# The high words of the weights written to PSUM by VectorE, their low parts added there, and the second group's pieces dealt out anew

## The chip, the cores and the metric

The kernel runs on one core of a Trainium2 chip. The metric is device microseconds of one execution; the time before is 1161.85 us, the median of 3 runs (1161.53 to 1161.90). Engines are called TensorE (PE, its weight loads PEld), VectorE (DVE), ScalarE (ACT), GpSimd (POOL) and SyncE (SP).

## The reference

A dynamic convolution of 7 taps with softmax weights, and behind it a two-layer net with a squared relu. All inputs are float32; the weights of the net come as float64 words (the kernel reads them as pairs of 32-bit words).

```python
w = softmax(weight_gen, axis=-1)                 # (4, 4096, 8 heads, 7 taps)
x = sum over taps k of w[..., k] * x[s - 6 + k]  # per head of 24 of the 192 columns
h = x.reshape(16384, 192) @ w_in                 # (16384, 2048)
out = (s * relu(h) ** 2 + b) @ w_out             # (16384, 192)
```

## The kernel before

The 16384 rows are worked in 32 groups of 512. Float32 accuracy is had from fp32r products: each operand is split into a high part, rounded to fp32r, and a low part, and three products (high x high, high x low, low x high) are added in PSUM.

**The weights.** They lie in 8 chunks (`wc_0` to `wc_7`), each with 256 rows of the hidden layer: 768 columns of `w_in` and `w_out`, high and low part. `load_weights(i)` brings the raw 64-bit words to a tile `r` (4 buffers). `convert(i)` is a generator of four steps, each started by `ahead(i, 1)`:
1. ScalarE takes the absolute value of the high words (L220);
2. VectorE clamps it, shifts it and puts the float32 together in place, in the high words (L223, L227, L231); ScalarE copies that to the high part `hi` (L235);
3. VectorE reads the high words again for the exponent (L238) and makes `v`, what the 64-bit word has beyond the high word, from the low words (L242);
4. TensorE adds three products with identity matrices in the PSUM tile `h1`: the float32 as it is (L252, a float32 product, which takes two passes in the trace), minus `hi` (L253), plus `v` (L254); ScalarE copies the sum to the low part `lo` (L255).

**The first group.** Its convolution has pieces of its own (row layout, ahead of the rest). Its net is worked in eight half-steps i = 0 to 7 (the loop at L671), while the weights are still being converted. A half-step issues: `mm1_pair` of chunk i on TensorE (into the PSUM tile `h0`), `relu2` on ScalarE (L546 relu, L548 square, L552 the high part `gh`) with step 4 of conversion i + 1 between the square and `gh`, steps 2 and 3 of conversion i + 2, step 1 of conversion i + 3, `mm2_pair` of chunk i - 1 on TensorE (L586), some pieces of the second group's convolution on VectorE (the table `beside`), and `low_g` on VectorE (L558, the low part `gl`, which `mm2_pair` of the next half-step reads).

**The second group's pieces** (`conv_pieces(1)`): softmax (three pieces), four products of taps with weights (L403, two heads by taps 0 to 3 and 4 to 6), five additions (L414, the last L422) that sum the 7 taps, the transposes (L433, L438), the split into high part (L445) and low part (L451). `split_lo` also issues a transfer within SBUF (`xb`).

**The other groups.** From `mm1_quad(4)` on (L693 and below) four steps to a group: `mm1_quad` (L535), `relu2`, `mm2_quad` of the step before (L604), pieces of the group after next, `low_g`, and once a group `scale` (L616, L622), which empties the sums `po` to `y`.

Every engine's work is issued in the order in which it is written (`manual_schedule`); an engine's instructions run in that order, and the program sets semaphores where one waits for another. PSUM tiles `h0` and `h1` have one buffer each.

The lines that set the order of the stage:

```python
beside = ((0, 1), (1, 3), (3, 4), (4, 5), (5, 7), (7, 8), (8, 14), (14, 15))
for i in range(NC):
    mm1_pair(n, p, ...)
    relu2(n, [p], lambda: ahead(i + 1, 1))
    ahead(i + 2, 2)
    ahead(i + 3, 1)
    mm2_pair((i - 1) // 2, (i - 1) % 2)
    run_pieces(1, *beside[i])
    low_g(n, p)
```

Of the kernel before, what the change touches and what calls it, by code (L numbers as in the profile page):

```python
# [7 lines left out]
F32 = mybir.dt.float32  # L8
F32R = mybir.dt.float32r
U32 = mybir.dt.uint32  # L10
AF = mybir.ActivationFunctionType
ALU = mybir.AluOpType
# [8 lines left out]
def dynamic_conv_then_relu2_mlp(  # L21
# [24 lines left out]
    nc = tc.nc  # L46
# [3 lines left out]
    P = 128  # L50
# [6 lines left out]
    T = 512  # L57
# [153 lines left out]
    def convert(i):  # L211


        r = raw_t.pop(i)
        hi, lo = wc[i][:, 0], wc[i][:, 1]
        low_w, high_w = r[:, :, 0], r[:, :, 1]
        fv = high_w.bitcast(F32)
        t = (rows if i % 2 else raw).tile([P, CW], U32, tag="t", name="t", bufs=1)
        tv = t.bitcast(F32)
        nc.scalar.activation(out=tv, in_=fv, func=AF.Abs)  # L220
        yield

        nc.vector.tensor_scalar(  # L223
            out=tv, in0=tv, scalar1=LEAST, scalar2=MOST, op0=ALU.max, op1=ALU.min
        )

        nc.vector.tensor_scalar(  # L227
            out=t, in0=t, scalar1=3, scalar2=0x3FFFFFFF,
            op0=ALU.logical_shift_left, op1=ALU.bitwise_and,
        )  # L230
        nc.vector.scalar_tensor_tensor(  # L231
            out=high_w, in0=high_w, scalar=0xC0000000, in1=t,
            op0=ALU.bitwise_and, op1=ALU.bitwise_or,
        )
        nc.scalar.copy(out=hi, in_=fv)  # L235
        yield

        nc.vector.tensor_scalar(  # L238
            out=t, in0=high_w, scalar1=0xFF800000, scalar2=None, op0=ALU.bitwise_and
        )  # L240
        v = raw.tile([P, CW], F32R, tag="v", name="v", bufs=2)
        nc.vector.scalar_tensor_tensor(  # L242
            out=v, in0=low_w, scalar=2.0 ** -52, in1=tv, op0=ALU.mult, op1=ALU.mult
        )
        yield

        ps = ps_h.tile([P, 2, T], F32, tag="h1", name="ph")
        n = CW // 2
        for a in range(2):
            c = slice(a * n, (a + 1) * n)  # L250
            o = ps[:, a, 0:n]
            nc.tensor.matmul(out=o, lhsT=eye_f, rhs=fv[:, c], start=True, stop=False)  # L252
            nc.tensor.matmul(out=o, lhsT=neg_eye, rhs=hi[:, c], start=False, stop=False)  # L253
            nc.tensor.matmul(out=o, lhsT=eye, rhs=v[:, c], start=False, stop=True)  # L254
        nc.scalar.copy(out=lo.rearrange("p (a n) -> p a n", a=2), in_=ps[:, :, 0:n])  # L255
        yield

    def awake():
# [46 lines left out]
    def conv_pieces(g):  # L305
# [110 lines left out]
                )  # L416
            return f

        def last_add():
            pr = st["pr"]  # L420
            acc = small.tile([P, J, FQ], F32, tag="acc", name="acc", bufs=1)
            nc.vector.tensor_tensor(out=acc, in0=pr[:, 0], in1=pr[:, 2], op=ALU.add)  # L422
            st["acc"] = acc
            xt_t.pop(g)

# [37 lines left out]
        if g == 0:  # L463
            return [
                softmax_a, exp, softmax_b, row_tails(0), row_tails(1), row_tails(2), row_tails(3), row_hi(1),
                row_firsts(0, 2), row_firsts(2, 4), row_firsts(4, 6), row_firsts(6, 7), row_hi(0), row_lo,
            ]
        return [
            softmax_a, exp, softmax_b,
# [72 lines left out]
    def relu2(n, ps=(0, 1), between=None):  # L542
        r = {}
        for p in ps:
            r[p] = act.tile([P, 2, T], F32, tag="r", name="r")
            nc.scalar.activation(out=r[p], in_=h_t.pop((n, p)), func=AF.Relu)  # L546
        for p in ps:
            nc.scalar.activation(out=r[p], in_=r[p], func=AF.Square)  # L548
            if between:
                between()  # L550
            gh = gp.tile([P, 2, T], F32R, tag="gh", name="gh")
            nc.scalar.copy(out=gh, in_=r[p])  # L552
            g_t[n, p] = r[p], gh
# [89 lines left out]
    with tc.manual_schedule():  # L643
        constants()
        nc.scalar.activation(out=bias[:, 0:1], in_=ones_f[:, 0:1], func=AF.Exp)
        load_rows(0)
        for i in range(4):
            load_weights(i)
        load_gen(1)

        parts = [convert(i) for i in range(NC)]

        def ahead(i, n):
            for _ in range(n if i < NC else 0):
                next(parts[i])

        awake()
        run_pieces(0, 0, 8)
        ahead(0, 1)
        run_pieces(0, 8, 13)  # L660
        ahead(0, 2)
        load_weights(4)
        load_x(1)
        nc.sync.dma_start(out=s_sb, in_=s.partition_broadcast(P))
        nc.sync.dma_start(out=b_sb, in_=b.partition_broadcast(P))
        run_pieces(0, 13, 14)
        ahead(1, 1)
        ahead(0, 1)

        beside = ((0, 1), (1, 3), (3, 4), (4, 5), (5, 7), (7, 8), (8, 14), (14, 15))  # L670
        for i in range(NC):  # L671
            n, p = divmod(i, 2)
            mm1_pair(n, p, (0, 2, 1) if i < 2 else (0, 1, 2))
            if i == 0:
                ahead(2, 1)
                ahead(1, 2)
                load_weights(5)
            relu2(n, [p], lambda: ahead(i + 1, 1))
            ahead(i + 2, 2)
            if i + 6 < NC:  # L680
                load_weights(i + 6)
            ahead(i + 3, 1)
            if i == NC - 1:
                sums = column_sums()
            if i > 0:
                mm2_pair((i - 1) // 2, (i - 1) % 2)
            run_pieces(1, *beside[i])
            if i == NC - 1:
                set_bias(sums)
            low_g(n, p)  # L690
            if i == 4:
                load(2)
        run_pieces(2, 0, 3)  # L693
        last = NG * NQ - 1
        for n in range(NQ, last + 1):
            g, k = divmod(n, NQ)
            if k == 0 and g + 2 < NG:
                load(g + 2)
            if k == 3:
                zeros_before(g + 2)  # L700
            mm1_quad(n)
            relu2(n)
            mm2_quad(n - 1, (1,) if n == NQ else (0, 1))
            a = (3, 5), (5, 8), (9, 14), (0, 2)
            run_pieces(g + 1 + k // 3, *a[k])
            if n == NQ:
                scale(0, (0, 2))
            low_g(n, 0)
            if k == 0 and n > NQ:
                scale(g - 1, (0, 2))  # L710
            low_g(n, 1)
            if k == 0:
                scale(g - 1, (1, 3))
                store(g - 1, 0, NT)
            a = (5, 5), (8, 9), (14, 15), (2, 3)
            run_pieces(g + 1 + k // 3, *a[k])

        for t in range(NT):
            mm2_pair(last, 0, [t], t == NT - 1)
        for t in range(NT):  # L720
            mm2_pair(last, 1, [t], t == NT - 1)
            scale(NG - 1, [t])
            store(NG - 1, t, t + 1)
# [30 lines left out]
```

## Time and profile before

| | us |
|---|---|
| median of 3 runs | 1161.85 |
| the profiled execution | 1160.27 |
| its span, first to last instruction | 1158.6 |
| TensorE busy in the span | 1146.5 (99%) |
| VectorE | 931.2 (80%) |
| ScalarE | 828.2 (71%) |
| GpSimd | 38.8 (3%) |

The shares are means over the whole span, of which the first 85 us or so hold the start, the conversions and the first group; the rest is the repeated steps of the other groups. The chain that ended last lies on TensorE for 97% of the span, most of it in L604 (47%) and L535 (45%); L252 has 1.0%. The granted TensorE clock is 0.998 of full speed (2.4 GHz).

### The profile page before, as it was taken

The numbers are of one execution on the slowest core, as the hardware profiler recorded it, in microseconds if no ns is written. First come the engines' busy times: TensorE is split into PE (matmuls) and PEld (weight loads), VectorE is DVE, ScalarE is ACT, GpSimd is POOL, SyncE is SP. The second block draws the span as 40 slices with busy tenths as digits, with TensorE's granted clock in tenths as the row PEclk, the third lists the DMA queues.
The fourth block names the chain that finished last, engine by engine and source line by source line (L and its number), as shares of the span: only waits on it lengthen the run. The fifth ranks groups of instructions, "written<-read, shape, count | busy, mean of one in ns | idle before, by whom it ended". The sixth has DMA issues, their size and how long they took to land.

```text
span 1158.6 us, 30256 instructions
## 1 busy us (share of the span) xinstructions
PE 1146.5 (99%) x12752; PEld 1128.9 (97%) x12752; DVE 931.2 (80%) x1356; ACT 828.2 (71%) x894; POOL 38.8 (3%) x86
## 2 busy tenths in 40 slices
PE   8999999999999999999999999999999999999997
PEld 6789999999999999999999999999999999999997
DVE  8998888877888877889877889877889877889843
ACT  5867677677677677677677777677777677776674
POOL 8300000000000000000000000000000000000000
PEclk9999999999999999999999999999999999999999
DMA  8422212222212222212222212222212222211110
GB/s 205 98 45 35 45 26 37 47 46 35 47 25 37 48 47 33 47 25 37 47 47 34 47 25 37 47 48 34 46 26 37 47 47 33 47 27 36 24 25 14
DMA packets 171867, 50.38 MB, mean 43 GB/s; under 512 B 160788, under 2 KB 164500, under 8 KB 171732
## 3 DMA queue, kind: packets, MB, share of 16 engines
q1 hardware_dynamic: 169684, 47.40, 22.5%
q8 instruction: 100, 1.64, 0.6%
q0 software_dynamic: 2048, 1.05, 0.4%
q14 instruction: 35, 0.29, 0.1%
HBM read 27.70 MB, written 12.58 MB: 35 GB/s over the span
## 4 chain that ended last, share of the span: by engine, by line
PE 97%; DMA 1%; DVE 1%; ACT 0%; POOL 0%; issue 0%; POOLq 0%
PE po L604 47%; PE ph L535 45%; PE po L586 2%; PE ph L517 2%; PE ph L252 1%; DMA r<-in_moe_w_in_dram 1%; POOL r L195 0%; PE ph L254 0%; PE ph L286 0%; PE ph L253 0%; ACT gh L552 0%; DVE u L616 0%; DVE y L622 0%; ACT r L548 0%; DVE gl L558 0%
## 5 line engine op out<-in xcount | busy, mean ns | idle before, releaser
L604 PE MATMUL po<-wc,gh 64*128 64x384 f32 x3952 | 584.0, 354 | 0.3 <-DVE y L622 0.3
L604 PE MATMUL po<-wc,gl 64*128 64x192 f32 x3952 | 573.3, 247 | 0.0
L604 PEld LDWEIGHTS po<-wc,gh 64*128 64x128 f32 x3952 | 568.2, 184 | 0.7 <-PE po L604 0.5
L604 PEld LDWEIGHTS po<-wc,gl 64*128 64x128 f32 x3952 | 564.4, 187 | 0.1
L558 DVE TENSOR_TENSOR gl<-r,gh 128x1024 fp32r<-128x1024 f32 x256 | 313.0, 1223 | 202.8 <-ACT gh L552 197.3
L546 ACT ACTIVATE r<-ph 128x1024 f32<-128x1024 f32 x256 | 249.2, 1024 | 293.8 <-PE ph L535 259.4
L535 PE MATMUL ph<-xa,wc 64*128 64x512 f32 x2976 | 381.3, 391 | 0.0
L535 PEld LDWEIGHTS ph<-xa,wc 64*128 64x128 f32 x2976 | 338.2, 184 | 1.0 <-issue 0.2
L552 ACT CAST gh<-r 128x1024 fp32r<-128x1024 f32 x256 | 269.1, 1051 | 7.9
L548 ACT ACTIVATE r<-r 128x1024 f32<-128x1024 f32 x256 | 270.7, 1057 | 0.3
L535 PE MATMUL ph<-xb,wc 64*128 64x512 f32 x1488 | 204.3, 386 | 0.0
L403 DVE TENSOR_TENSOR pr<-xt,w 128x1536 f32<-128x1536 f32 (+1 forms) x124 | 187.4, 1551 | 1.6 <-DMA xt<-in_x_dram 0.4
L535 PEld LDWEIGHTS ph<-xb,wc 64*128 64x128 f32 x1488 | 178.8, 184 | 0.5
L414 DVE TENSOR_TENSOR pr<-pr 128x1536 f32<-128x1536 f32 (+1 forms) x124 | 140.7, 1155 | 2.1
L616 DVE SCALAR_TENSOR_TENSOR u<-po,s_sb,bias 128x192 f32<-128x192 f32 x128 | 47.2, 409 | 1.0 <-PE po L586 1.0
L622 DVE SCALAR_TENSOR_TENSOR y<-po,s_sb,u 128x192 f32<-128x192 f32 x128 | 47.1, 407 | 0.1
L159 POOL MEMSET xt<- 1x288 f32 x16 | 5.3, 332 | 1023.1 <-DVE xT L433 1022.5
L195 POOL DMA_DIRECT2D r<-in_moe_w_in_dram x64 | 32.7, 518 | 6.0 <-DMA r<-in_moe_w_in_dram 3.7
L422 DVE TENSOR_TENSOR acc<-pr 128x768 f32<-128x768 f32 x31 | 29.7, 958 | 1.1
L433 DVE STREAM_TRANSPOSE xT<-acc 128x128 f32<-128x128 f32 x124 | 27.6, 281 | 1.1
L438 DVE STREAM_TRANSPOSE xT<-acc 128x128 f32<-128x128 f32 x124 | 26.3, 270 | 0.0
L451 DVE TENSOR_TENSOR xa<-xT,xa 128x512 fp32r<-128x512 f32 x31 | 21.2, 685 | 0.0
(60 smaller groups left out, 371.8 us busy)
## 6 DMA issues: line engine op xcount, KB each, us to landing
xt<-in_x_dram SPq DMA_DIRECT2D x120, 132.0 KB, 3.7
out_dram<-y SPq DMA_DIRECT2D x124, 96.0 KB, 1.9
xb<-xb SPq DMA_DIRECT2D x124, 64.0 KB, 2.3
wg<-in_weight_gen_dram SPq DMA_DIRECT2D x124, 28.0 KB, 2.6
r<-in_moe_w_out_dram SPq DMA_DIRECT2D x8, 384.0 KB, 4.7
r<-in_moe_w_in_dram SPq DMA_DIRECT2D x32, 64.0 KB, 3.7
r<-in_moe_w_in_dram POOLq DMA_DIRECT2D x64, 16.0 KB, 4.1
xr<-in_x_dram SPq DMA_DIRECT2D x1, 672.0 KB, 4.7
```

Source lines behind the costliest of these rows:

```text
L195: nc.gpsimd.dma_start(out=rw[q * 32 + a * TAIL:q * 32 + (a + 1) * TAIL, CB * 2:CO * 2], in_=bass.AP(src.tensor, src.offset, [[F * 2, TAIL] ...
L403: nc.vector.tensor_tensor(out=pr[:, k0:k1, :, h * G:(h + 1) * G], in0=bass.AP(xs.tensor, xs.offset, [xs.ap[0], [FQ, n], [FQ, J], [1, G]]), ...
L414: nc.vector.tensor_tensor(out=pr[:, o:o + n], in0=pr[:, o:o + n], in1=pr[:, a:a + n], op=ALU.add)
L422: nc.vector.tensor_tensor(out=acc, in0=pr[:, 0], in1=pr[:, 2], op=ALU.add)
L535: nc.tensor.matmul(out=h_t[n, p][:, j], lhsT=w1(2 * k + p, part, block, j, rows), rhs=v[rows], start=(at < 2 and c == 0), stop=(at >= 4 an ...
L546: nc.scalar.activation(out=r[p], in_=h_t.pop((n, p)), func=AF.Relu)
L548: nc.scalar.activation(out=r[p], in_=r[p], func=AF.Square)
L552: nc.scalar.copy(out=gh, in_=r[p])
L558: nc.vector.tensor_tensor(out=gl, in0=sq, in1=gh.bitcast(F32), op=ALU.subtract)
L604: nc.tensor.matmul(**m)
L616: nc.vector.scalar_tensor_tensor(out=u[i], in0=o_t[g][tiles[i]][:, 1, :], scalar=s_sb, in1=bias, op0=ALU.mult, op1=ALU.add,)
L622: nc.vector.scalar_tensor_tensor(out=y[:, t], in0=o_t[g][t][:, 0, :], scalar=s_sb, in1=u[i - 1], op0=ALU.mult, op1=ALU.add,)
```

## The change

For conversions 2 to 7 the PSUM tile `h1` is taken in step 2 already: VectorE writes the float32 of the high word there instead of in place; ScalarE's copy to `hi` and VectorE's second read take it from there; and in step 4 only the two fp32r products are left, which add to what VectorE wrote. Conversions 0 and 1 stay as they were. In `relu2` step 4 of the next conversion comes ahead of the square. The second group gets a list of pieces of its own: taps 2 and 3 are added to taps 0 and 1 by a transfer that adds (on GpSimd's queue, 768 KB within SBUF), the other additions follow in another order, and `beside` deals the pieces out anew: the half-steps 2 and 5 have none, 3 and 4 one product each, 6 two products and two additions, 7 the rest.

```diff
@@ -220,6 +220,12 @@
         nc.scalar.activation(out=tv, in_=fv, func=AF.Abs)
         yield
 
+        n = CW // 2
+        added = i > 1
+
+        def halves(v):
+            return v.rearrange("p (a n) -> p a n", a=2)
+
         nc.vector.tensor_scalar(
             out=tv, in0=tv, scalar1=LEAST, scalar2=MOST, op0=ALU.max, op1=ALU.min
         )
@@ -228,15 +234,20 @@
             out=t, in0=t, scalar1=3, scalar2=0x3FFFFFFF,
             op0=ALU.logical_shift_left, op1=ALU.bitwise_and,
         )
+        if added:
+            ps = ps_h.tile([P, 2, T], F32, tag="h1", name="ph")
+            fv = ps[:, :, 0:n]
+        else:
+            fv = halves(fv)
         nc.vector.scalar_tensor_tensor(
-            out=high_w, in0=high_w, scalar=0xC0000000, in1=t,
+            out=fv.bitcast(U32), in0=halves(high_w), scalar=0xC0000000, in1=halves(t),
             op0=ALU.bitwise_and, op1=ALU.bitwise_or,
         )
-        nc.scalar.copy(out=hi, in_=fv)
+        nc.scalar.copy(out=halves(hi), in_=fv)
         yield
 
         nc.vector.tensor_scalar(
-            out=t, in0=high_w, scalar1=0xFF800000, scalar2=None, op0=ALU.bitwise_and
+            out=halves(t), in0=fv.bitcast(U32), scalar1=0xFF800000, scalar2=None, op0=ALU.bitwise_and
         )
         v = raw.tile([P, CW], F32R, tag="v", name="v", bufs=2)
         nc.vector.scalar_tensor_tensor(
@@ -244,15 +255,16 @@
         )
         yield
 
-        ps = ps_h.tile([P, 2, T], F32, tag="h1", name="ph")
-        n = CW // 2
+        if not added:
+            ps = ps_h.tile([P, 2, T], F32, tag="h1", name="ph")
         for a in range(2):
             c = slice(a * n, (a + 1) * n)
             o = ps[:, a, 0:n]
-            nc.tensor.matmul(out=o, lhsT=eye_f, rhs=fv[:, c], start=True, stop=False)
-            nc.tensor.matmul(out=o, lhsT=neg_eye, rhs=hi[:, c], start=False, stop=False)
-            nc.tensor.matmul(out=o, lhsT=eye, rhs=v[:, c], start=False, stop=True)
-        nc.scalar.copy(out=lo.rearrange("p (a n) -> p a n", a=2), in_=ps[:, :, 0:n])
+            if not added:
+                nc.tensor.matmul(out=o, lhsT=eye_f, rhs=fv[:, a], start=True, stop=False)
+            nc.tensor.matmul(out=o, lhsT=neg_eye, rhs=hi[:, c], start=False, stop=False, skip_group_check=added)
+            nc.tensor.matmul(out=o, lhsT=eye, rhs=v[:, c], start=False, stop=True, skip_group_check=added)
+        nc.scalar.copy(out=halves(lo), in_=ps[:, :, 0:n])
         yield
 
     def awake():
@@ -416,10 +428,16 @@
                 )
             return f
 
-        def last_add():
+        def add_by_queue(o, a, n):
+            def f():
+                pr = st["pr"]
+                nc.gpsimd.dma_start(out=pr[:, o:o + n], in_=pr[:, a:a + n], accum_op=ALU.add)
+            return f
+
+        def last_add(a=2):
             pr = st["pr"]
             acc = small.tile([P, J, FQ], F32, tag="acc", name="acc", bufs=1)
-            nc.vector.tensor_tensor(out=acc, in0=pr[:, 0], in1=pr[:, 2], op=ALU.add)
+            nc.vector.tensor_tensor(out=acc, in0=pr[:, 0], in1=pr[:, a], op=ALU.add)
             st["acc"] = acc
             xt_t.pop(g)
 
@@ -464,6 +482,12 @@
             return [
                 softmax_a, exp, softmax_b, row_tails(0), row_tails(1), row_tails(2), row_tails(3), row_hi(1),
                 row_firsts(0, 2), row_firsts(2, 4), row_firsts(4, 6), row_firsts(6, 7), row_hi(0), row_lo,
+            ]
+        if g == 1:
+            return [
+                softmax_a, exp, softmax_b, products(0, 0, 4), products(1, 0, 4), add_by_queue(0, 2, 2),
+                products(0, 4, 7), products(1, 4, 7), add(0, 4, 2), add(0, 6), lambda: last_add(1),
+                transposes, split_hi, split_lo,
             ]
         return [
             softmax_a, exp, softmax_b,
@@ -545,9 +569,9 @@
             r[p] = act.tile([P, 2, T], F32, tag="r", name="r")
             nc.scalar.activation(out=r[p], in_=h_t.pop((n, p)), func=AF.Relu)
         for p in ps:
-            nc.scalar.activation(out=r[p], in_=r[p], func=AF.Square)
             if between:
                 between()
+            nc.scalar.activation(out=r[p], in_=r[p], func=AF.Square)
             gh = gp.tile([P, 2, T], F32R, tag="gh", name="gh")
             nc.scalar.copy(out=gh, in_=r[p])
             g_t[n, p] = r[p], gh
@@ -667,7 +691,7 @@
         ahead(1, 1)
         ahead(0, 1)
 
-        beside = ((0, 1), (1, 3), (3, 4), (4, 5), (5, 7), (7, 8), (8, 14), (14, 15))
+        beside = ((0, 1), (1, 3), (3, 3), (3, 4), (4, 6), (6, 6), (6, 10), (10, 14))
         for i in range(NC):
             n, p = divmod(i, 2)
             mm1_pair(n, p, (0, 2, 1) if i < 2 else (0, 1, 2))
```

In the program as built, VectorE's round with one piece before (conversion 4, half-step 2; `r` is the raw tile, `t` scratch, `pr` the products, in square brackets the semaphores waited for, by the engine or DMA queue that sets them):

```order
L558 TENSOR_TENSOR gl<-r,gh 128x1024
L223 TENSOR_SCALAR t<-t 128x768
L227 TENSOR_SCALAR t<-t 128x768 [waits DVE_49]
L231 SCALAR_TENSOR_TENSOR r<-r,t 128x768 [waits DMASW6_49,DMASW7_49,DMASW5_49,DMAHW3_49,DMASW4_49,DMAHW4_49,DMASW3_49,DMAHW5_49,DMASW2_49,DMAHW6_49,DMASW1_49,DMAHW7_49,DMASW0_49,DVE_49]
L238 TENSOR_SCALAR t<-r 128x768 [waits DVE_49]
L242 SCALAR_TENSOR_TENSOR v<-r,t 128x768 [waits DVE_49,PE_49]
L403 TENSOR_TENSOR pr<-xt,w 128x64x24 [waits DMAHW2_49,DMAHW3_49,DMAHW1_49,DMAHW0_49]
L558 TENSOR_TENSOR gl<-r,gh 128x1024 [waits Activation_49]
```

and such a round after the change (conversion 5, half-step 3; the lines are those of the changed kernel, L229 to L253 for L223 to L242, L415 for L403, L582 for L558):

```order
L582 TENSOR_TENSOR gl<-r,gh 128x1024
L229 TENSOR_SCALAR t<-t 128x768 [waits Activation_49]
L233 TENSOR_SCALAR t<-t 128x768 [waits DVE_49]
L242 SCALAR_TENSOR_TENSOR ph<-r,t 128x2x384 [waits DMASW6_49,DMASW5_49,DMASW7_49,DMASW4_49,DMAHW0_49,DMASW3_49,DMAHW1_49,DMASW2_49,DMAHW2_49,DMASW1_49,DMAHW6_49,DMASW0_49,DMAHW7_49,DVE_49,Activation_49]
L249 TENSOR_SCALAR t<-ph 128x768 [waits Activation_49]
L253 SCALAR_TENSOR_TENSOR v<-r,t 128x768 [waits DVE_49]
L415 TENSOR_TENSOR pr<-xt,w 128x64x24 [waits DMAHW3_49]
L582 TENSOR_TENSOR gl<-r,gh 128x1024
```

The five instructions stand as before; the third of them, L242, writes the PSUM tile `ph` and waits for ScalarE, and the fourth, L249, reads `ph` and waits for ScalarE where it waited for VectorE.

ScalarE's round of a half-step before (half-step 1):

```order
L546 ACTIVATE r<-ph 128x1024 [waits PE_49]
L548 ACTIVATE r<-r 128x1024 [waits Activation_49]
L255 CAST wc_93<-ph 128x768 [waits PE_49]
L552 CAST gh<-r 128x1024 [waits Activation_49]
L235 CAST wc_94<-r 128x768 [waits DVE_49]
```

and after:

```order
L570 ACTIVATE r<-ph 128x1024 [waits PE_49]
L267 CAST wc_93<-ph 128x768 [waits DVE_49,PE_49]
L574 ACTIVATE r<-r 128x1024 [waits Activation_49]
L576 CAST gh<-r 128x1024 [waits Activation_49]
L246 CAST wc_94<-ph 128x768 [waits DVE_49]
```

The copy of the low part (L267, L255 before) has moved ahead of the square (L574, L548 before); the copy of the next conversion's high part (L246, L235 before) stays behind `gh`.

## Rows read from the trace of the kernel before

**Rows 1.** Windows: busy us of PE, PEld, DVE, ACT, POOL (instructions), PEclk, DMA share, GB/s
```profile
5.00:7.50 2.50, 1.35 (x5) 0.70 (x4) 1.25 (x5) 0.56 (x1) 0.94 (x2) 1.00 1.00 288
41.00:48.00 7.00, 7.00 (x40) 5.48 (x39) 6.72 (x8) 5.76 (x7) 0.00 (x0) 1.00 0.48 87
85.00:1150.00 1065.00, 1065.00 (x12269) 1064.70 (x12270) 852.87 (x1229) 769.16 (x825) 5.32 (x16) 1.00 0.22 38
```
**Rows 2.** Chain that ended last, one conversion on TensorE (start us, us, what)
```profile
46.91 0.87 PE ph L252 x2
...
48.13 0.68 PE ph L252 x2
```
**Rows 3.** Timeline of VectorE, one round (start us, us, instruction; idle before, releaser)
```profile
32.87 0.39 DVE L385 TENSOR_REDUCE sm<-e 128x32 f32<-128x224 f32 x1 [0.66 <-ACT e L380]
...
34.21 1.22 DVE L558 TENSOR_TENSOR gl<-r,gh 128x1024 fp32r<-128x1024 f32 x1
...
36.59 0.96 DVE L231 SCALAR_TENSOR_TENSOR r<-r,t 128x768 uint32<-128x768 uint32 x1
37.59 0.56 DVE L238 TENSOR_SCALAR t<-r 128x768 uint32<-128x768 uint32 x1
...
39.13 1.75 DVE L403 TENSOR_TENSOR pr<-xt,w 128x1536 f32<-128x1536 f32 x1
40.80 1.22 DVE L558 TENSOR_TENSOR gl<-r,gh 128x1024 fp32r<-128x1024 f32 x1
```
**Rows 4.** Timelines of ScalarE, then of VectorE, at the conversion of chunk 2
```profile
23.98 0.80 ACT L255 CAST wc<-ph 128x768 fp32r<-128x768 f32 x1
24.68 1.05 ACT L552 CAST gh<-r 128x1024 fp32r<-128x1024 f32 x1
25.63 0.89 ACT L235 CAST wc<-r 128x768 fp32r<-128x768 f32 x1
...
25.01 0.56 DVE L238 TENSOR_SCALAR t<-r 128x768 uint32<-128x768 uint32 x1
...
27.27 1.22 DVE L558 TENSOR_TENSOR gl<-r,gh 128x1024 fp32r<-128x1024 f32 x1
```
**Rows 5.** Groups of VectorE by line and shape, 0 to 112 us (busy us, mean ns)
```profile
L403 DVE TENSOR_TENSOR pr<-xt,w 128x1152 f32<-128x1152 f32 x4 | 5.2, 1351 | 0.0
...
L295 DVE SCALAR_TENSOR_TENSOR bias<-ph,b_sb,cs 128x192 f32<-128x192 f32 x1 | 0.4, 419 | 0.0
L294 DVE TENSOR_SCALAR cs<-ph,b_sb 128x192 f32<-128x192 f32 x1 | 0.4, 418 | 0.3 <-PE ph L286 0.3
```
**Rows 6.** Timeline of VectorE, the second group's last pieces
```profile
52.32 2.62 DVE L403 TENSOR_TENSOR pr<-xt,w 128x1152 f32<-128x1152 f32 x2
54.86 1.22 DVE L558 TENSOR_TENSOR gl<-r,gh 128x1024 fp32r<-128x1024 f32 x1
...
59.78 1.75 DVE L414 TENSOR_TENSOR pr<-pr 128x1536 f32<-128x1536 f32 x1
...
62.59 2.81 DVE L414 TENSOR_TENSOR pr<-pr 128x768 f32<-128x768 f32 x3
65.44 0.96 DVE L422 TENSOR_TENSOR acc<-pr 128x768 f32<-128x768 f32 x1
...
70.67 0.42 DVE L294 TENSOR_SCALAR cs<-ph,b_sb 128x192 f32<-128x192 f32 x1 [0.27 <-PE ph L286]
...
71.88 1.23 DVE L558 TENSOR_TENSOR gl<-r,gh 128x1024 fp32r<-128x1024 f32 x1 [0.35 <-ACT gh L552]
```
**Rows 7.** Timelines of VectorE and TensorE, the first quad step to TensorE's last wait
```profile
72.84 3.02 PE L535 MATMUL ph<-xa,wc 64*128 64x512 f32 x24
...
82.63 1.23 DVE L558 TENSOR_TENSOR gl<-r,gh 128x1024 fp32r<-128x1024 f32 x1 [0.82 <-ACT gh L552]
...
84.98 0.73 PE L604 MATMUL po<-wc,gh 64*128 64x384 f32 x2 [0.28 <-DVE y L622]
```
**Rows 8.** DMA issues by line (KB each, median us to landing)
```profile
xr<-in_x_dram SPq DMA_DIRECT2D x1, 672.0 KB, 4.7
```

## Prediction

> **What bounds the kernel now.** I read the windows by stage first. From 85 us to the end TensorE is busy in all of the time, VectorE in 80% of it [rows 1]. That stretch is TensorE's alone, and the change leaves it as it is; it can only start sooner or later. So what counts is when TensorE gets there, and the change lies wholly ahead of it, in the stage of eight half-steps (i = 0 to 7) that convert the weights beside the first group's work.
>
> In that stage, at 41 to 48 us, TensorE is busy 7.00 of 7.00 us and VectorE 6.72 [rows 1]. Both look full, so I went on to the chain that ended last and to VectorE's timeline. The chain runs over TensorE here, and a conversion's two float32 products (L252) stand in it with 0.87 and 0.68 us [rows 2]. VectorE's timeline shows that it keeps the same pace without a hole: from one `gl` (L558) to the next it takes 40.80 - 34.21 = 6.59 us, filled by the five instructions of one conversion, one piece of the second group's convolution (39.13 to 40.80, 1.67 us) and the `gl` itself [rows 3]. **Two engines are at their limit at once**; a cut on one of them alone brings nothing.
>
> **What the change takes from TensorE.** Six conversions (2 to 7) lose L252: 6 x (0.87 + 0.68) = 9.3 us. This is worth something only as far as VectorE can follow.
>
> **What it does to VectorE.** The program's order shows a new wait: the read L249 (L238 before) now waits for ScalarE, where it waited for VectorE's own L242 (before L231). What it waits for is ScalarE's copy of the high word from the same PSUM tile, which stands between the two in the source. The trace shows no two engines reading one PSUM tile at once, so by rows alone I take the wait at its word, as the program has it. The Trainium skill ("PSUM — Partial Sum Buffer", PSUM bank collisions raise a hardware error) says why it is there: two engines may not touch one bank at the same time, two reads included.
>
> - *The hole.* Before, L231 starts at 36.59 and L238 at 37.59: 0.96 of work and 0.04 of handover [rows 3]. Now the copy comes between: 0.04, the copy, 0.04. A copy of 128x768 from PSUM takes 0.80 (L255 [rows 4]); from SBUF it took 0.89 (L235 [rows 4]), the upper end. Cost 0.84 us in each conversion, if ScalarE is free when L242 ends.
> - *The read.* L238 takes 0.56 from SBUF [rows 3]. No row has a 768-wide read of this kind from PSUM. Below stands 0.56, no price at all. Above: over 192 columns from PSUM the same operation (L294) takes 418 ns, as long as the two-input L295 beside it with 419 [rows 5], and a two-input instruction of 768 takes 0.96 (L231 [rows 3]); adding 576 columns at 1.05 ns (L403: 1.75 us over 1536 [rows 3], 1.35 over 1152 [rows 5]) gives 1.02. I take 0.98, by L294, the only read of this kind: + 0.42.
> - *The write* of L242 into PSUM has no row. Below, no two-input instruction of 768 columns takes under 0.96 (L422 [rows 6]); above, 1.02 as for the read. I take 0.96.
>
> The Trainium skill ("VectorE: DVE Perf Modes", Why PSUM operands drop a tier) speaks against this change too: a float32 operand in PSUM keeps such an instruction at one column per cycle. With that page's cycle formulas (section on the TRN2 errata) the read would be an estimated 0.93 us, and the sum about 0.3 us smaller.
>
> A conversion thus costs VectorE 1.26 us more. Against it stand the sums: five additions before (1.75, three in 2.81, 0.96 [rows 6]: 5.5), three now (1.75, 0.95, 0.96: 3.66), since the transfer adds two taps to two others: 1.9 us less.
>
> **The start.** `h1` is one tile, and L242 of conversion 2 now writes it, so it waits for the copy L255 of conversion 1. That copy starts at 23.98 and takes 0.80, for it waits for TensorE's products, which don't move. ScalarE then does the square first (24.68, the copy's successor before, plus 1.06 and 0.04), then `gh` at 25.78, and 0.95 later, at 26.73, the high word's copy, which ends at 27.53. L249 starts at 27.57 instead of 25.01 [rows 4]: + 2.56; with the dearer read + 2.98. `gl` of i = 0, before at 27.27 [rows 4], comes at 30.25.
>
> **The rounds** from one `gl` to the next, without a piece 6.59 - 1.67 + 1.26 = 6.18, with one 7.85:
> - 0 to 1: no piece, but the softmax's tail (32.87 to 34.21 [rows 3], 1.34): 7.5. Its wait of 0.66 goes.
> - 1 to 2 and 4 to 5: no piece: 6.2 each.
> - 2 to 3 and 3 to 4: one piece: 7.85 each.
> - 5 to 6: no conversion left, two products (52.32 to 54.86, 2.54), additions of 1.75 and 0.95, `gl` with 1.2: 6.4 [rows 6].
> - 6 to 7: `gl` and the last addition, transposes, split and bias, as from 65.44 to 71.88 before, less the waits of 0.27 and 0.35, plus some 0.1 for the split's copies that `gl` no longer covers: 5.9 [rows 6].
>
> Together 47.9 us, before 71.88 - 27.27 = 44.6. With the start, `gl` of i = 7 is 6.3 us late, at 78.2.
>
> **The hand-over to TensorE's stretch.** From there VectorE has the third group's softmax and products, then scales the first group's sums, and TensorE's last wait of the run hangs on it: L604 at 84.98, for `y` [rows 7]. Before, 71.88 to 84.98 is 13.1 us, in which a `gl` waited 0.82 for ScalarE [rows 7]. Late as it is, VectorE no longer waits there, and 12.3 remain: 90.5, that is **+ 5.5 us**. TensorE on its own gets there at nearly the same time: its first quad step, at 72.84 before [rows 7], needs the second group's split, which now ends the bias's two instructions of 0.42 [rows 5] ahead of `gl` of 7, at 77.3: + 4.5, and it starts with stalls.
>
> The profiled execution took 1160.27 us (span 1158.6 us and 1.67 around it); it becomes 1165.8. The median of the three runs shown, 1161.85, stands 1.58 above it, so I forecast 1161.85 + 5.5 = **1167.4 us**.
>
> Costed at nothing: the products' wait for VectorE's read, hidden by the later wait for `gl`; the earlier copy L255, which only trades places with the square; the transfer's issue on GpSimd, which has no work after 40 us. The **adding transfer** moves 768 KB within SBUF. It is issued after the product of round 3 to 4 (59.6) and needed after the two products of round 5 to 6 (69.5): 9.9 us. A load of 672 KB lands in 4.7 us [rows 8]. If reading both sides doubles it, 4.7 x 1536 / 672 = 10.7, near the edge; I take it as hidden.
>
> With the read at 0.56 the sum is 5.5 - 6 x 0.42 = 3.0; with the write at 1.02, the read at 1.02 and the copy at 0.89, 5.5 + 6 x (0.06 + 0.04 + 0.09) = 6.6. The mechanism's own range is 1164.9 to 1168.5.
>
> **Rivals.** Something under 0.2% (2.3 us) can't be told from no change.
> - *Faster.* The hole doesn't arise, because ScalarE's copy comes before VectorE wants to read, and the read is as cheap as from SBUF. What is left for VectorE are gains: 1.9 us of additions, and its waits for the other engines in the stage, which now come earlier (0.66 at L385, 0.27 and 0.35, 0.82 [rows 3, 6, 7]: 2.1). TensorE's 9.3 are worth no more than these, for VectorE's rounds are full. 1161.85 - 4.0 = 1157.9. It decides in the conversions: at 4.0 / 6 = 0.67 us of extra cost in each nothing is gained, under 0.28 it is over 0.2%. For it speaks that TensorE stands in the whole chain of that stretch [rows 2]; against it that the wait is in the program, and the copy alone has 0.80. 7%.
> - *Within 0.2%.* Only the hole shows: the read at 0.56, and the start's delay soaked up: 6 x 0.84 - 4.0 = 1.0: 1162.9. Against it speaks L294. 9%.
> - *The transfer is late.* The place is L426's wait in round 5 to 6; it decides at 9.9 us. Should it take 15, 5 more: 1172.5. Against it the row of the load above. 8%.
> - *The clock falls,* since TensorE now idles in each round. In rows, 5.0 to 7.5 us has TensorE busy 1.35 of 2.5 us at a granted 1.00, the upper level, 2.4 GHz [rows 1]. At 1.2 GHz its 5.3 us of a round (6.9 less 1.55) would be 10.6 and set the pace, some 3.6 more in each of six rounds, 21.6: 1189. The Trainium skill ("TensorE: Matmul & The Clock Gate", Part 1) holds that an idle array loses its clock; that row of half idleness disagrees so far. 2%.
>
> **How the numbers follow.** My forecast, slower by 3.0 to 6.6, has 74%. The range takes its bounds, the case within 0.2%, and a transfer that is late by 1 us or 2: 1162.6 to 1169.5. Faster 0.07, same 0.09, slower 0.84.
>
> **What would show it.** Right: L249 idle about 0.9 us each time, released by ScalarE's copy; L249 near 0.98 us; TensorE waiting for `gl` at the second products in the rounds with a piece, and for VectorE at the first conversion by 2 us; rounds of 6.2 and 7.9; TensorE's last wait near 90. Wrong: TensorE without waits and rounds below 6 us (then VectorE was not the limit), L249 at 0.56, or a wait for the transfer in L426.

## The result and the profile after

The changed kernel takes **1168.94 us** (median of 4 runs, 1168.15 to 1170.26), the kernel before 1161.88 on the same chip (4 runs, 1161.53 to 1162.07). The ratio is 1.0062 with a 95% interval of 1.0048 to 1.0076: 7.2 us more (5.6 to 8.8). The profiled execution of the changed kernel took 1168.15 us, its span 1166.4. In the runs further down, one of e6's (3882.7 us) and one of the kernel before in each set (2224 us) were slow ones and stay out of the ratios. Line numbers below are those of the changed kernel (L242 for L231 before, L249 for L238, L253 for L242, L582 for L558, L628 for L604).

TensorE's long stretch is unchanged. From its last wait to the end of the span there are 1166.4 - 92.77 = 1073.6 us, before 1158.6 - 84.98 = 1073.6 [rows 7]. So the whole difference lies ahead of that wait, as the prediction had it, and the wait has come 7.8 us later. The windows of the changed kernel (busy us of PE, PEld, DVE, ACT, POOL, then PEclk, DMA share, GB/s) answer to [rows 1]:

```profile
40.00:60.00 20.00, 17.44 (x95) 12.93 (x93) 16.19 (x18) 15.48 (x19) 1.52 (x3) 1.00 0.31 57
85.00:1150.00 1065.00, 1064.73 (x12268) 1064.26 (x12267) 856.84 (x1237) 770.96 (x828) 5.30 (x16) 1.00 0.22 38
```

Before, TensorE and VectorE were both full in the stage of the half-steps. Now neither is: of 20 us TensorE works 17.4 and VectorE 16.2. One hands work to the other, with a wait in between. VectorE's timeline of one round with a piece (start us, us, instruction; idle before, releaser) answers to [rows 3] and shows where:

```profile
52.74 1.22 DVE L582 TENSOR_TENSOR gl<-r,gh 128x1024 fp32r<-128x1024 f32 x1
...
55.15 0.97 DVE L242 SCALAR_TENSOR_TENSOR ph<-r,t 128x768 uint32<-128x768 uint32 x1
56.99 0.96 DVE L249 TENSOR_SCALAR t<-ph 128x768 uint32<-128x768 uint32 x1 [0.87 <-ACT wc L246]
57.98 0.96 DVE L253 SCALAR_TENSOR_TENSOR v<-r,t 128x768 fp32r<-128x768 uint32 x1
58.86 1.75 DVE L415 TENSOR_TENSOR pr<-xt,w 128x1536 f32<-128x1536 f32 x1
60.52 1.22 DVE L582 TENSOR_TENSOR gl<-r,gh 128x1024 fp32r<-128x1024 f32 x1
```

L249 starts 1.84 after L242, before 1.00 [rows 3], and takes 0.96 instead of 0.56. The round has 7.78 us, before 6.59. Over the six conversions (VectorE's groups by line and shape, 0 to 112 us: busy us, mean ns, idle before) the wait adds up to 6.9 us:

```profile
L242 DVE SCALAR_TENSOR_TENSOR ph<-r,t 128x768 uint32<-128x768 uint32 x6 | 5.8, 967 | 2.0 <-DMA r<-in_moe_w_out_dram 1.3
L249 DVE TENSOR_SCALAR t<-ph 128x768 uint32<-128x768 uint32 x6 | 5.7, 958 | 6.9 <-ACT wc L246 6.9
```

TensorE in turn waits for VectorE. Its timeline shows the first conversion, two of the rounds, the first quad step, and the last wait of the run (which answers to [rows 7]):

```profile
29.17 0.66 PE L265 MATMUL ph<-wc,neg_eye 128*128 128x384 f32 x1 [2.20 <-DVE t L249]
...
54.01 0.36 PE L610 MATMUL po<-wc,gl 128*128 128x192 f32 x1 [1.83 <-DVE gl L582]
...
61.80 0.36 PE L610 MATMUL po<-wc,gl 128*128 128x192 f32 x1 [1.83 <-DVE gl L582]
...
78.73 3.15 PE L559 MATMUL ph<-xa,wc 64*128 64x512 f32 x24
...
83.38 1.65 PE L559 MATMUL ph<-xb,wc 64*128 64x512 f32 x11 [1.31 <-DMA xb<-xb]
...
92.77 0.73 PE L628 MATMUL po<-wc,gh 64*128 64x384 f32 x2 [0.27 <-DVE y L646]
```

So far this is the prediction's mechanism. The theory to test: **VectorE's hole behind L242 and its dearer read set the time; the products on VectorE's data and the adding transfer cost nothing.** Rivals: the second group's new pieces or their transfer cost the time; the earlier place of the copy to `lo` does; TensorE's clock does, for its windows show a thing that the kernel before has only behind TensorE's last product (0.51 at 1154 to 1156 us):

```profile
30.00:32.00 2.00, 1.72 (x5) 1.21 (x5) 1.97 (x5) 0.57 (x1) 1.56 (x4) 0.50 0.78 189
32.00:34.00 2.00, 2.00 (x8) 2.00 (x9) 1.86 (x3) 1.97 (x3) 2.00 (x5) 0.50 0.73 245
...
64.00:66.00 2.00, 2.00 (x8) 1.81 (x8) 1.19 (x2) 0.74 (x1) 0.00 (x0) 0.50 0.98 197
```

The granted clock (PEclk) is 0.50 there, the lower level of 1.2 GHz, at 30 to 34 and at 64 to 66 us.

### The profile page after: what moved, and what is told of

It is laid out like the page before. It is cut to its first block, busy times and chain, and to the rows that moved or that the text cites. A ratio compares the mean times of both kernels' runs of the same rounds, so it can differ in the third digit from the quotient of the medians.

```text
span 1166.4 us, 30170 instructions
## 1 busy us (share of the span) xinstructions
PE 1145.9 (98%) x12728; PEld 1129.5 (97%) x12728; DVE 931.8 (80%) x1354; ACT 827.2 (71%) x894; POOL 38.9 (3%) x87
## 3 DMA queue, kind: packets, MB, share of 16 engines
q0 software_dynamic: 2192, 1.84, 0.8%
## 4 chain that ended last, share of the span: by engine, by line
PE 93%; DVE 2%; DMA 2%; ACT 1%; POOL 1%; issue 0%; SPq 0%; ACTq 0%; POOLq 0%; DVEq 0%
PE po L628 47%; PE ph L559 44%; DMA r<-in_moe_w_in_dram 2%; PE po L610 1%; PE ph L541 1%; POOL r L195 0%; ACT r L574 0%; DVE gl L582 0%; ACT gh L576 0%; DVE t L249 0%; DMA xb<-xb 0%; DVE pr L415 0%; ACT wc L246 0%; DVE v L253 0%; DVE u L640 0%
## 5 line engine op out<-in xcount | busy, mean ns | idle before, releaser
L628 PE MATMUL po<-wc,gh 64*128 64x384 f32 x3952 | 580.3, 354 | 0.3 <-DVE y L646 0.3
L628 PE MATMUL po<-wc,gl 64*128 64x192 f32 x3952 | 569.9, 247 | 0.0
L628 PEld LDWEIGHTS po<-wc,gl 64*128 64x128 f32 x3952 | 560.8, 187 | 0.0
L628 PEld LDWEIGHTS po<-wc,gh 64*128 64x128 f32 x3952 | 554.9, 184 | 0.6 <-PE po L628 0.5
L582 DVE TENSOR_TENSOR gl<-r,gh 128x1024 fp32r<-128x1024 f32 x256 | 313.0, 1223 | 203.1 <-ACT gh L576 197.7
L559 PEld LDWEIGHTS ph<-xa,wc 64*128 64x128 f32 x2976 | 334.8, 184 | 0.7 <-issue 0.4
L574 ACT ACTIVATE r<-r 128x1024 f32<-128x1024 f32 x256 | 270.7, 1057 | 0.0
L559 PE MATMUL ph<-xb,wc 64*128 64x512 f32 x1488 | 200.9, 386 | 1.3 <-DMA xb<-xb 1.3
L415 DVE TENSOR_TENSOR pr<-xt,w 128x1536 f32<-128x1536 f32 (+1 forms) x124 | 187.4, 1551 | 1.2
L559 PEld LDWEIGHTS ph<-xb,wc 64*128 64x128 f32 x1488 | 175.2, 184 | 1.9 <-DMA xb<-xb 1.8
L610 PE MATMUL po<-wc,gh 128*128 128x384 f32 x72 | 24.1, 392 | 0.0
```

Of the source, the lines that this page charges most:

```text
L415: nc.vector.tensor_tensor(out=pr[:, k0:k1, :, h * G:(h + 1) * G], in0=bass.AP(xs.tensor, xs.offset, [xs.ap[0], [FQ, n], [FQ, J], [1, G]]), ...
L559: nc.tensor.matmul(out=h_t[n, p][:, j], lhsT=w1(2 * k + p, part, block, j, rows), rhs=v[rows], start=(at < 2 and c == 0), stop=(at >= 4 an ...
L582: nc.vector.tensor_tensor(out=gl, in0=sq, in1=gh.bitcast(F32), op=ALU.subtract)
L610: nc.tensor.matmul(**m)
L628: nc.tensor.matmul(**m)
```

## The experiments

Ratios are to the kernel before on the same chip, with 95% intervals; the line numbers of a kernel with the copy moved are up to 3 higher.

| kernel | median us (runs) | before | ratio |
|---|---|---|---|
| changed kernel | 1168.94 (4) | 1161.88 | 1.0062, 1.0048 to 1.0076 |
| e1, copy behind the read | 1162.90 (11) | 1161.69 | 1.0010, 1.0001 to 1.0019 |
| e2, new pieces alone | 1162.07 (11) | 1161.69 | 1.0006, 0.9997 to 1.0016 |
| e3, conversions alone | 1170.85 (5) | 1161.69 | 1.0080, 1.0067 to 1.0093 |
| e4, square first again | 1167.29 (5) | 1161.69 | 1.0050, 1.0037 to 1.0063 |
| e5, read from SBUF | 1160.69 (11) | 1161.59 | 0.9992, 0.9983 to 1.0000 |
| e6, two chunks | 1159.64 (11) | 1161.59 | 0.9985, 0.9976 to 0.9994 |
| e7, TensorE kept busy | 1166.21 (5) | 1161.59 | 1.0044, 1.0030 to 1.0058 |
| e8, three chunks | 1159.69 (11) | 1161.59 | 0.9985, 0.9976 to 0.9994 |

### e1: ScalarE's copy behind VectorE's read

For conversions 2 to 7 the copy to `hi` is written behind L249, so VectorE reads first and ScalarE waits.

```diff
-        nc.scalar.copy(out=halves(hi), in_=fv)
+        if not added:
+            nc.scalar.copy(out=halves(hi), in_=fv)
         yield
...
+        if added:
+            nc.scalar.copy(out=halves(hi), in_=fv)
```

> The changed kernel with ScalarE's copy of the high word behind VectorE's second read (L249) instead of ahead of it, in conversions 2 to 7; all the work stays. Theory: VectorE's hole is the largest part. L249 then follows L242 at once, the idle 6.9 us before L249 go, a round without a piece takes 6.2 - 0.85 = 5.3 to 5.8 (ScalarE or TensorE may set it), one with a piece 7.0, and gl of half-step 0 comes some 1.8 earlier; in all 5 to 6 us less than the changed kernel's 1168.9: 1163 to 1164, still 1 to 2 above the kernel before. Rival, the clock: the granted clock at 0.50 around 30 to 35 and 62 to 66 us is what costs, and the hole is only where VectorE waits anyway; then less than 2 us go, and the time stays over 1167.

Measured: 1162.90 us, just under the expected 1163, and + 1.2 us over the kernel before (0.1 to 2.2). Two lines that swap places give back 6.0 of the 7.2 us. VectorE's groups by shape and, behind them, its timeline:

```profile
L242 DVE SCALAR_TENSOR_TENSOR ph<-r,t 128x768 uint32<-128x768 uint32 x6 | 5.8, 967 | 3.8 <-ACT wc L270 1.7 <-DMA r<-in_moe_w_in_dram 1.6
L250 DVE TENSOR_SCALAR t<-ph 128x768 uint32<-128x768 uint32 x6 | 5.7, 958 | 0.2
```

```profile
46.10 0.97 DVE L242 SCALAR_TENSOR_TENSOR ph<-r,t 128x768 uint32<-128x768 uint32 x1 [1.73 <-ACT wc L270]
```

The 6.9 us of idle time before the read are 0.2 now; the read's length is the same. A new wait of 1.73 shows up once, at 46.10: with one tile `h1`, the next L242 must wait until ScalarE has copied the sum before it to `lo`.

The clock fell in e1 too, once, to 0.50 from 39 to 42 us. The window and TensorE's timeline:

```profile
36.00:40.00 4.00, 2.15 (x12) 1.92 (x10) 3.76 (x7) 3.04 (x4) 3.17 (x6) 0.84 0.82 191
```

```profile
38.08 0.35 PE L613 MATMUL po<-wc,gl 128*128 128x192 f32 x1 [1.85 <-DVE gl L585]
```

The group of products that starts there took 3.50 us (38.08 to 41.58), the next one 2.07 (45.22 to 47.29), and ScalarE's relu and copy L270, for which L242 waits at 46.10, come behind it. So an estimated 1.4 us of that wait, the difference of the two groups, are the clock's and not the order's; no run tests this. The gain lies in three places: between the two profiled executions (5.3 us apart) the first `gl` is 1.47 earlier (29.18), the rounds are 2.62 shorter, and the hand-over to TensorE's stretch is 1.21 shorter.

### e2 and e3: the two halves of the change apart

e2 keeps the conversions and the place of the square of before and takes only the new pieces with their transfer. e3 is the opposite: the changed kernel with the pieces and `beside` of before.

```diff
e2:
-        added = i > 1
+        added = False
...
+            nc.scalar.activation(out=r[p], in_=r[p], func=AF.Square)
             if between:
                 between()
-            nc.scalar.activation(out=r[p], in_=r[p], func=AF.Square)
e3:
-        if g == 1:
-            return [
-                softmax_a, exp, softmax_b, products(0, 0, 4), products(1, 0, 4), add_by_queue(0, 2, 2),
-                products(0, 4, 7), products(1, 4, 7), add(0, 4, 2), add(0, 6), lambda: last_add(1),
-                transposes, split_hi, split_lo,
-            ]
...
-        beside = ((0, 1), (1, 3), (3, 3), (3, 4), (4, 6), (6, 6), (6, 10), (10, 14))
+        beside = ((0, 1), (1, 3), (3, 4), (4, 5), (5, 7), (7, 8), (8, 14), (14, 15))
```

> The kernel before with only the second group's new pieces, their new places beside the half-steps and the adding transfer; conversions and the order around the square as before. Theory of two limits: VectorE has 1.9 us less, but TensorE still has its float32 products and its round of 6.8 to 6.9; nearly nothing is gained: 1160.5 to 1162, TensorE without waits of more than 0.5 us in the stage. Rival, that the pieces or the transfer are what costs: the time rises by 2 us or more, with a wait before the additions or the split.

> The changed kernel with the second group's pieces and their places as before (five additions on VectorE, no adding transfer). Theory: every round of VectorE's carries a piece, and each of the six conversions costs 1.26 more; from gl of half-step 0 to that of 7 it takes 44.6 + 6 x 1.26 - 0.7 = 51.5 against 48.6 in the changed kernel: 2 to 3 us more than that, 1171 to 1172. Rival, that the new pieces cost by themselves: the time falls below 1168.

Measured: e2 + 0.7 us (- 0.3 to 1.9), e3 + 9.3 us (7.8 to 10.8), each within 0.2 us of its expected range, but outside it (1162.07 and 1170.85). So the pieces and the transfer aren't what costs; put onto the conversions they give 2.1 us back (e3 against the changed kernel, intervals that overlap), close to the 1.9 of the prediction's additions. That it is so close proves little: e3's clock stood at 0.50 for longer (three stretches, some 20 us in all, against some 10). Alone, the pieces and the transfer give nothing, and e2's VectorE timeline shows why:

```profile
71.89 0.69 DVE L469 TENSOR_TENSOR xb<-xT,xb 128x512 fp32r<-128x512 f32 x1 [2.74 <-ACT xb L463]
```

TensorE still has L252's work there and in the half-steps it never waits for more than 0.3 us. What VectorE saves turns into a wait of 2.74 at the end of the stage. e3 is the case with the longest waits of TensorE for `gl` (total us, times, longest):

```profile
PE po L604 <- DVE gl L576: 5.4, 3, 2.7
```

### e4: the square ahead of the copy to `lo` again

```diff
+            nc.scalar.activation(out=r[p], in_=r[p], func=AF.Square)
             if between:
                 between()
-            nc.scalar.activation(out=r[p], in_=r[p], func=AF.Square)
```

> The changed kernel with the square ahead of the next conversion's step 4 again, as before the change. Theory: in the start the square then fills ScalarE's wait for TensorE (1.28 us), so that gh and the high word's copy come 1.1 earlier and with them L249 of conversion 2; in the rounds the low part's copy comes up to 1 us later, just about when VectorE wants h1: 1167 to 1169, no clear gain. Rival: the low part's copy becomes VectorE's next wait (L242 waits for ScalarE in each round), and the time rises over 1171.

Measured: 1167.29 us, + 5.8 us (4.3 to 7.3), 1.4 below the changed kernel, with intervals that overlap. The earlier copy isn't the cause of the loss, and in this order it doesn't help either. VectorE's waits:

```profile
DVE t L249 <- ACT wc L246: 5.2, 6, 0.9
DVE ph L242 <- DMA r<-in_moe_w_in_dram: 2.9, 2, 2.3
```

L249 waits 0.86 or 0.87 in all six conversions, 5.2 instead of 6.9 us: this is the bare hole, with ScalarE free each time. In conversion 2 the wait only moves to L242, ahead of the read (the profile names a load, but L242 starts 0.03 us after the copy L267).

### e5: the second read from SBUF

VectorE reads the raw high word in SBUF for the exponent, so L249 needs neither PSUM nor ScalarE. The rest stays: L242 writes PSUM, and the products add to it. The exponents are then not the right ones, so e5 only prices the read.

```diff
-            out=halves(t), in0=fv.bitcast(U32), scalar1=0xFF800000, scalar2=None, op0=ALU.bitwise_and
+            out=halves(t), in0=halves(high_w), scalar1=0xFF800000, scalar2=None, op0=ALU.bitwise_and
```

> The changed kernel, but VectorE's second read (L249) takes the raw high word from the raw tile in SBUF in place of the finished one in PSUM, so the exponents are not the right ones; every instruction stays. It takes away the hole and the read's price together. Theory: L249 takes 0.56 again, without a wait; against the copy moved behind the read (1162.9) another 6 x 0.40 = 2.4 us of VectorE go, of which ScalarE's and TensorE's own rounds (5.7 and 5.3) leave about 2: 1160 to 1161.5, at or under the kernel before. Rival: if writing to PSUM, or the products on what VectorE wrote, cost by themselves, it stays at 1162.5 or above.

Measured: 1160.69 us, - 0.9 us (- 2.0 to 0.0), 2.1 below e1. From the rows, the read's price is 6 x (0.96 - 0.56) = 2.4. The two agree in part by chance, for e5 differs from e1 in more than the read: L242's wait for the copy to `lo` is 0.52 instead of 1.73, and the hand-over is 1.2 longer (70.69 to 84.19 against 75.20 to 87.47). The write to PSUM and the products on VectorE's data cost nothing that shows. Its groups by shape and TensorE's waits:

```profile
L249 DVE TENSOR_SCALAR t<-r 128x768 uint32<-128x768 uint32 x8 | 4.5, 560 | 0.3
```

```profile
PE po L610 <- DVE gl L582: 3.4, 4, 1.4
...
PE ph L559 <- DMA xb<-xb: 1.3, 1, 1.3
```

This is all that is left of L252's 9.3 us when hole and read are both gone: TensorE is ahead and waits for VectorE, whose rounds with a piece are still as long as before (46.92 to 53.48 us, 6.56).

### e7: TensorE kept busy while it waits

The changed kernel with idle products of 128 columns into an unused part of a PSUM bank: 30 ahead of conversion 2, and 26 behind the first product of `mm2_pair` in half-steps 4 and 5.

```diff
+    def fill(g, times, start=False):
+        for _ in range(times):
+            nc.tensor.matmul(
+                out=bank_t[g][3][:, 2 * D:T], lhsT=eye, rhs=wc[0][:, 0, 0:P],
+                start=start, stop=start, skip_group_check=True,
+            )
...
+            if i == 1:
+                outputs(0)
+                fill(0, 30, True)
...
-            mm2_pair((i - 1) // 2, (i - 1) % 2)
+            mm2_pair((i - 1) // 2, (i - 1) % 2, fills=26 if i in (4, 5) else 0)
```

> The changed kernel with idle products of 128 columns for TensorE (identity times weights, into unused columns of a PSUM bank): 30 ahead of conversion 2 and 26 behind the first product of the half-steps 4 and 5, where it otherwise waits 1.8 to 2.2 us for VectorE. VectorE's and ScalarE's work stays. It asks what the fallen clock costs: the granted clock should stay at 1.00 at 30 to 35 and 62 to 66 us. Theory: VectorE sets the pace and the clock cost under 1 us: 1167.5 to 1169. Rival, the clock is the larger part of the 7 us: under 1166.

Measured: 1166.21 us, + 5.1 us (3.5 to 6.7): 2.1 below the changed kernel by the ratios (2.7 by the medians), with intervals that overlap. By its time alone it suits neither expectation well, so its rows have to be asked. Windows, then VectorE's and TensorE's timelines:

```profile
32.00:34.00 2.00, 2.00 (x15) 1.95 (x15) 1.42 (x2) 1.97 (x3) 1.64 (x5) 1.00 0.88 259
...
64.00:66.00 2.00, 2.00 (x12) 1.48 (x13) 1.97 (x3) 0.00 (x0) 0.00 (x0) 1.00 0.55 107
```

```profile
30.17 1.22 DVE L582 TENSOR_TENSOR gl<-r,gh 128x1024 fp32r<-128x1024 f32 x1
...
41.84 0.96 DVE L249 TENSOR_SCALAR t<-ph 128x768 uint32<-128x768 uint32 x1 [0.87 <-ACT wc L246]
...
78.04 1.22 DVE L582 TENSOR_TENSOR gl<-r,gh 128x1024 fp32r<-128x1024 f32 x1
```

```profile
81.10 1.66 PE L559 MATMUL ph<-xb,wc 64*128 64x512 f32 x11 [0.29 <-DMA xb<-xb]
...
90.50 0.73 PE L640 MATMUL po<-wc,gh 64*128 64x384 f32 x2 [0.27 <-DVE y L658]
```

The clock is 1.00 in all those windows, and the last wait comes at 90.50 instead of 92.77. Of these 2.27 us the clock explains only a part. The first `gl` is 0.48 earlier; the instructions that put it there lie before the first idle product (the copy to `lo` of conversion 1 starts at 24.01 here, at 24.50 in the changed kernel). The waits of L249 in conversions 3 and 4 shrink from 0.99 and 1.22 to 0.86 and 0.87, 0.48 together: these stand right behind the products at the lower clock, which kept ScalarE late. The last round is 0.29 shorter, and TensorE's wait for the `xb` transfer 1.02 shorter. That last one need not be the clock's: e5 has the same 1.3 with the clock at 1.00 in every window from 20 to 90 us. So by these rows the clock costs the changed kernel about 0.5 us in the rounds, 0.8 with the last round. Whether the `xb` transfer lands sooner because of the idle products or by chance stays open.

### e6 and e8: the new way for some chunks

Since TensorE and VectorE were both full before, the new way should pay where it takes from TensorE about what it adds to VectorE. e6 takes it for conversions 4 and 7 alone, e8 for 4, 6 and 7; both with e1's order, the square first and the new pieces.

```diff
-        added = i > 1
+        added = i in (4, 7)
```

> A version built on the theory of two limits: the new way for the conversions 4 and 7 alone, which run in the two half-steps without pieces of the second group (there VectorE has 1.9 us to spare), ScalarE's copy behind the read, the square first as in the kernel before, the second group's new pieces kept. TensorE loses 2 x 1.55 = 3.1 us, VectorE gets 2 x 0.40 more and keeps its 1.9 us of additions saved. Theory: 1.5 to 2.5 us under the kernel before: 1159.3 to 1160.3. Rival, that the new way costs wherever it is put: 1161.5 or more.

> As the version with the conversions 4 and 7, and conversion 6 as well, whose half-step has a piece. Theory: there VectorE is the limit, so the third buys nothing: within 0.5 us of the version with two. Rival, that TensorE alone sets the pace: 1.5 us less than with two.

Measured: 1159.64 and 1159.69 us, both - 1.7 us (- 2.8 to - 0.7). They beat both kernels by little, though with 11 runs each the interval excludes 1. e6's stage (its profiled execution took 1161.18, the upper end of its runs, with a granted clock of 0.50 at 10 to 12 us, ahead of the stage; so this is read for the waits and not for the time) and TensorE's wait in e8:

```profile
40.00:60.00 20.00, 20.00 (x111) 15.90 (x110) 18.73 (x22) 16.22 (x18) 4.06 (x8) 1.00 0.50 94
```

```profile
55.65 0.36 PE L613 MATMUL po<-wc,gl 128*128 128x192 f32 x1 [1.06 <-DVE gl L585]
```

With two chunks TensorE stays full, at a clock of 1.00. The third saves it another 1.5 us of L252 and pays with 1.06 of waiting for `gl`; the time is the same.

## Why the prediction was right, and where its sum was short

The direction and the mechanism held, and so did the place. The forecast of + 5.5 us was 1.7 short of the 7.2 measured. That is more than the mechanism's own upper end (6.6 us, 1168.5): 1168.94 lies in the range only because the range had been widened for a late adding transfer, which was not late. To that extent the range held by luck. Point by point, against the profiled execution (last wait at 92.77, forecast 90.5):

- **The hole.** Forecast 0.84; the bare hole is 0.87, and e1 shows that it is most of the loss: 6.0 us went with it, what hangs on it included. The Trainium skill ("PSUM — Partial Sum Buffer", PSUM bank collisions raise a hardware error) gave the reason for the wait: two reads of one bank by two engines are kept apart. The trace agrees (L246 ends at 56.95, L249 starts at 56.99), and e1 shows that either engine may be the first.
- **The read.** Forecast 0.98, measured 0.958 (the prediction's own sum gave 1.02; it has no step from there to 0.98); the Trainium skill's cycle formulas ("VectorE: DVE Perf Modes", section on the TRN2 errata), an estimated 0.93 in the prediction, were as near. The rows price it at 2.4 us; e5 is 2.1 below e1.
- **The write.** Forecast 0.96, measured 0.967.
- **The adding transfer.** Forecast hidden, with 10.7 us as its upper estimate. It took 5.8 (the page's DMA issues below), and the addition that needs it started without a wait.

```profile
pr<-pr POOLq DMA_DIRECT2D x1, 768.0 KB, 5.8
```

```profile
70.44 2.75 DVE L426 TENSOR_TENSOR pr<-pr 128x1536 f32<-128x1536 f32 x2
```

- **The start,** forecast at 30.25, came at 30.65. The step that failed is "it waits for TensorE's products, which don't move". ScalarE's and VectorE's rows of conversion 2 answer to [rows 4]:

```profile
24.50 0.80 ACT L267 CAST wc<-ph 128x768 fp32r<-128x768 f32 x1 [1.28 <-PE ph L266]
...
27.24 0.79 ACT L246 CAST wc<-ph 128x768 fp32r<-128x768 f32 x1
```

```profile
25.33 0.97 DVE L242 SCALAR_TENSOR_TENSOR ph<-r,t 128x768 uint32<-128x768 uint32 x1 [1.32 <-DMA r<-in_moe_w_out_dram]
28.06 0.96 DVE L249 TENSOR_SCALAR t<-ph 128x768 uint32<-128x768 uint32 x1 [1.77 <-ACT wc L246]
```

  The copy L267 starts at 24.50 instead of 23.98, and L242 begins 0.03 after its end (the releaser named is a DMA, but the copy was the last). The work ahead of it had shifted by half a microsecond long before, in a stretch that the change doesn't touch: in 28 products that sum taps of the first group (TensorE's timelines, before and after):

```profile
7.42 4.80 PE L320 MATMUL px<-eye_f,pb 128*128 128x128 f32 x28 [1.15 <-ACT pb L339]
7.30 5.37 PE L332 MATMUL px<-eye_f,pb 128*128 128x128 f32 x28 [0.93 <-ACT pb L351]
```

  In e7 the same products took 3.8 us (7.20 to 11.01), the copy started at 24.01, and `gl` came at 30.17. So this miss is chance and not the change's. From there on the order was as forecast.
- **The rounds,** forecast 47.9 together, took 48.6 (`gl` at 30.65 and 79.29). The condition "if ScalarE is free when L242 ends" failed in three conversions: L249 waited 0.99, 1.22 and 1.15 instead of 0.87, 0.75 more, and the round from i = 6 to 7 has 0.41 of waiting for ScalarE's copy of the split. The rounds from 3 to 4 and 4 to 5, where ScalarE was free, took 7.78 and 6.12 against a forecast of 7.85 and 6.2.
- **The hand-over,** forecast 12.3, took 13.5 (79.29 to 92.77): the largest miss of the sum. The step that failed is "late as it is, VectorE no longer waits there". The prediction saw that TensorE's first quad step would start with stalls and gave them no price. TensorE came to the `xb` half about 4.0 us after that transfer was issued (78.02), before about 6.0 (issued at 69.83, needed 3 us after 72.84 [rows 7]), and waited 1.31 for it. The transfer was slower too: its four parts took 2.4 to 3.9 us to land, before and in e7 2.3 to 2.4, and with that e7 waited only 0.29; why it was slower, no run shows. So ScalarE's `gh` was late and VectorE waited 0.29 and 0.81 for it after all. Where TensorE did not wait for `xb`, the 12.3 came out: in e1 from 75.20 to 87.47, in e6 from 73.47 to 85.76.
- **The clock** had 2%, as a rival that costs 3.6 us in each round. It fell, but in two stretches and not throughout, and by e7's rows cost 0.5 to 0.8 us (in e1 an estimated 1.4). The sentence that failed is "that row of half idleness disagrees so far": one early stretch at a granted 1.00 said nothing of this stage, and that 1.00 is itself in doubt (the last section). The Trainium skill ("TensorE: Matmul & The Clock Gate", Part 1) was right that an idle array loses its clock; the rival's price was wrong, since the clock was low for some 10 us only, and VectorE sets the pace of these rounds and hides most of the slower products.

From kernel to kernel, then: the order of read and copy takes 6.0 away (e1), the cheaper read another 2.1 (e5), and - 0.9 is left for all that the change gains (TensorE's six L252, and the additions). That these make + 7.2 is no proof, for they are differences along one row of kernels, and each holds what followed from it (the clock, the `xb` transfer). As the prediction argued, what is taken from one of two full engines brings nothing by itself: e2 (VectorE relieved alone) came out even, and e5 (TensorE relieved, VectorE's price gone) gained 0.9 us of a possible 9.3. Which of e5's remaining waits keeps it from more wasn't taken apart.

## What to carry to other kernels

If two engines must read the same PSUM tile one after the other, let the engine that sets the pace read first: here that was two lines in another order, and 6 us. Where two engines are full at once, trade work only as far as both stay full (two chunks of six here, - 1.7 us), since beyond that each relief turns into a wait. And price what stands behind the stage too: a transfer that had landed some 1.6 us before it was needed became the next wait when the work around it was dealt out anew.

## What the runs showed of the hardware

- **TensorE's granted clock halved in the middle of the stage.** It stood at 0.50 (1.2 GHz) from 30 to 34 us, after an idle time of 2.20 us that ended at 29.17, and was back at 1.00 from 36 us on; it fell again between 62 and 64, after 1.83 us of idle time before 61.80. Another idle time of 1.83 us, before 54.01, was followed by no fall; in e1 one of 1.85, before 38.08, was followed by one. In the first stretch one `mm2_pair` took 31.93 to 35.79 us, 3.86 instead of 2.22 in the next round but one (45.94 to 48.16). With idle products in the gaps (e7) the clock stayed at 1.00.
- **The granted clock of the first rows is in doubt.** From 7 to 12 us the rows of the changed kernel say 1.00, but the 28 products L332 there have a median of 421 ns, and those of the same shape behind them 272. In e6, where the rows say 0.50 at 10 to 12 us, the same products also take 421; in e7 they take 273. Why the row and the products differ, no run shows; the products' own length is the safer reading there.
- **An adding transfer within SBUF** of 768 KB landed in 5.8 us (5.7 to 6.4 over the runs that have it), where a load of 672 KB took 4.6 to 4.7 [rows 8]: reading both sides did not double it. Its issue kept GpSimd for 0.92 us.
- **VectorE writes PSUM as fast as SBUF** (967 against 959 ns for L242's two forms, 768 columns), while the one-input read from PSUM takes 958 against 560.
